# Row-tiled attention scores: two steps of 576 columns with an ordering fence, in place of three steps

## The chip, the core and the metric

One Trainium2 chip (trn2), one core. The metric is the device time of one execution in microseconds. The program runs on a single core, where most executions of one kernel agree within 0.3%, and the granted TensorE clock was 1.00 in the profiles before.

The profile's names: PE is the matrix engine and PEld its weight loads, ACT is ScalarE, DVE is VectorE, POOL is GpSimd, and a q behind a name (ACTq) means that engine's sequencer. `L279` is line 279 of the kernel at hand.

## The reference, cut to what matters

```python
k_p = k.reshape(B, H, 72, 8, 64).mean(axis=3)          # B=8, H=8, 576 tokens pooled to 72 keys
v_p = v.reshape(B, H, 72, 8, 64).mean(axis=3)
scores = q @ k_p.transpose(0, 1, 3, 2) / 8             # 576 x 72 per head
attn = softmax(scores)                                 # exp, then divided by the sum
x = attn @ v_p                                         # -> (B, 576, 512)
h = relu(x.T @ w_tok1) @ w_tok2 ; u = x + h.T          # mixing over tokens
out = u + relu(u @ w_ch1) @ w_ch2                      # mixing over channels, most of the work
```

## The kernel before

The PE runs `unit n`: the channel mixing of batch n in 48 steps, of two matmuls of 512 columns each (24 of `w_ch1`, 24 of `w_ch2`). Steps of the next batches are slipped in behind them by hand-written tables, such as `22: ">s0"`: behind step 22 of unit n, the score step s0 of batch n+2. `av`, `at`, `u`, `t` or `T` are the value, token-mixing and transposing steps that follow.

A score step multiplies four heads at once. The 64 numbers of a head are two halves (`db`) of 32, so each of the four row tiles (strips of 32 rows of the array, each with weights of its own) works on one head (`l`), in two rounds that accumulate:

```python
def score4(gs, n0, n):                       # before: s0, s1: one group of 4 heads, tokens 0 to 511
    pss = [ps_two.tile([P, 2, 512], FP32, name="p2") for _ in range(2)]        # s2: both groups, the last 64
    for i, g in enumerate(gs):
        for db in range(2):
            for l in range(4):
                quad = slice(l * 32, (l + 1) * 32)
                nc.tensor.matmul(out=pss[l // 2][0:SP, l % 2, i * n:(i + 1) * n], lhsT=st["kD"][quad, g, db, :],
                                 rhs=st["qD"][quad, g, db, n0:n0 + n],
                                 start=(db == 0), stop=(db == 1), tile_position=(l * 32, 0))
    ...
    for a in range(2):
        nc.scalar.activation(out=exv[...], in_=pss[a][...], func=AF.Exp, scale=scale)
```

PSUM is the memory that matmuls write. The kernel uses eight banks of it: two double ones (`p2`), three rotating single ones (`p1`, also for all large matmul groups) and one for transposes (`pt`). An eviction is an ACT instruction that reads a finished group of `w_ch1` out of its bank into the tile `GT`.

The softmax here doesn't subtract the row's maximum and nothing guards it: scores larger than these inputs give would overflow.

Of the kernel before, what the change touches and what calls it, by code (L numbers as in the profile page):

```python
# [8 lines left out]
FP32 = mybir.dt.float32  # L9
BF16 = mybir.dt.bfloat16  # L10
AF = mybir.ActivationFunctionType
# [3 lines left out]
DVE = mybir.EngineType.DVE  # L15
ACT = mybir.EngineType.Activation
SYNC = mybir.EngineType.SP


@with_exitstack  # L20
def kernel(
# [14 lines left out]
    nc = tc.nc  # L36
    B, H, S, D = q.shape
    P = 128
    POOL = 8
    SP = S // POOL  # L40
    BP, BR = 64, S // 64
# [8 lines left out]
    scale = 1.0 / (D ** 0.5) / POOL  # L50
# [9 lines left out]
    ps_one = ctx.enter_context(tc.tile_pool(name="ps_one", bufs=3, space=bass.MemoryType.PSUM))  # L60
    ps_two = ctx.enter_context(tc.tile_pool(name="ps_two", bufs=2, space=bass.MemoryType.PSUM))
    ps_tr = ctx.enter_context(tc.tile_pool(name="ps_tr", bufs=1, space=bass.MemoryType.PSUM))
# [93 lines left out]
    def batch_steps(b):  # L156

        par, first = b % 2, b == 0
        st = {}
# [85 lines left out]
        def qD(g, db):  # L245
            def go():
                st["qraw"] = quarters(loaded[b, "q"])
                nc.vector.transpose(  # L248
                    out=late("qD")[:, g, db].rearrange("m (r j u) -> m u r j", u=2, r=BR),
                    in_=st["qraw"][:, g].rearrange("m (u r d) -> m u r d", u=2, d=D)[:, :, :, db * 32:(db + 1) * 32])  # L250
            return go

        def score4(gs, n0, n):
            def go():
                pss = [ps_two.tile([P, 2, 512], FP32, name="p2") for _ in range(2)]
# [7 lines that stand above are left out]
                exv = st["ex"][:, 0:H * S].rearrange("j (g a l n) -> j a l g n", g=2, a=2, l=2)  # L263
                for a in range(2):
                    nc.scalar.activation(  # L265
                        out=exv[:, a, :, gs.start:gs.stop, n0:n0 + n],
                        in_=pss[a][0:SP, :, 0:len(gs) * n].rearrange("j l (g n) -> j l g n", n=n), func=AF.Exp, scale=scale)
            return go

        def score(hp, odd):  # L270
            n = OD if odd else EV

            def go():
                ps = ps_two.tile([P, 2, 512], FP32, name="p2")
                exv = st["ex"][:, 0:H * S].rearrange("j (h n) -> j h n", h=H)[:, 2 * hp:2 * hp + 2]
                for hl in range(2):
                    h = 2 * hp + hl
                    keys = slice(h * SP, (h + 1) * SP)
                    nc.tensor.matmul(out=ps[0:SP, hl, 0:n], lhsT=kT[:, odd, keys], rhs=qT0[:, hp, hl, 0:n],  # L279
                                     start=True, stop=True)  # L280
                dst = exv.rearrange("j h (r p) -> j h r p", p=BP)[:, :, odd:BR:2, :]
                src = ps[0:SP, :, 0:n].rearrange("j h (r p) -> j h r p", p=BP)
                nc.scalar.activation(out=dst, in_=src, func=AF.Exp, scale=scale)
            return go
# [182 lines left out]
        name = {"kpT": kpT}  # L467
# [5 lines left out]
        for hp in range(HP):  # L473
            name[f"kp{hp}"], name[f"kt{hp}"] = kp2(hp), kt2(hp)
            name[f"q{hp}"], name[f"o{hp}"], name[f"e{hp}"] = qT(hp), score(hp, 1), score(hp, 0)
        for i in range(4):
            name[f"Q{i}"] = qD(i // 2, i % 2)
        name["s0"], name["s1"], name["s2"] = (score4(range(0, 1), 0, 8 * BP), score4(range(1, 2), 0, 8 * BP),
                                              score4(range(2), 8 * BP, BP))
        for c in range(5):  # L480
            name[f"av{c}"], name[f"u{c}"], name[f"t{c}"] = av(c), u(c), uT(c)
            name[f"T{c}"] = blocks(c)
# [22 lines left out]
    def unit_steps(n, st):  # L505
# [36 lines left out]
        for a in range(2):  # L542
# [7 lines left out]
            for half in range(2):  # L550
# [9 lines left out]
             11: "lv3", 12: "kpT", 14: "s0", 15: "v1", 19: "s1", 25: "s2", 26: "av0", 27: "av1", 29: "av2",  # L560
             30: ">K1 av4", 31: "av3", 33: "at1", 34: "at0", 35: ">K0", 36: ">V1 u0", 37: "u1", 39: "t0 >V0",
             40: "u2", 41: "t1 u4 u3", 42: "t2", 44: "t3", 46: "t4"}
    SECOND = {0: ">K1 Q0 lq3 kpT Q1 Q2", 1: "lv3", 3: "s0 lk3 >V0", 4: ">K0", 6: "Q3 >V1", 8: "s1", 13: "s2",
              16: "av1 av0", 19: "av2", 20: "av3", 22: "av4", 24: "at1 at0", 26: "u0", 28: ">Q0", 29: "u1", 30: "t0",
              31: "u2", 32: "t1", 33: "u3 t2", 35: "t3", 36: ">Q1", 37: ">kpT", 38: "lq4", 39: ">s0 >Q2",
              40: ">Q3 lv4", 44: ">s1", 45: "lk4"}
    THIRD = {0: ">V0 >K1", 1: "s2", 2: ">K0 >V1", 3: "av0 av1", 6: "av3", 7: "av2", 9: "av4", 10: "at0",
             12: "at1 >Q0", 15: "u0", 16: "u1", 17: "u2 t0", 18: "u4", 19: "t1", 21: "u3", 22: "t2", 24: ">Q1",
             25: "t3", 27: "lq4 >kpT", 28: "lv4", 29: "lk4 >Q3 >s0 >Q2", 32: "t4", 33: ">s1", 38: ">s2", 40: ">av0",
             41: ">av2", 43: ">av1", 45: ">av3", 47: ">av4"}  # L570
    FOURTH = {0: "M4 u4 >K1", 1: "at0 at1 >K0", 3: "u0 >V0", 5: "u1 M0", 6: ">V1", 7: "u2", 8: "u3 M2", 9: "M",
              15: ">kpT >Q1", 17: ">Q0", 22: "lq4", 25: ">Q2", 26: ">s0", 27: "T0", 28: ">Q3 lk4 lv4", 29: "T1",
              32: ">s1 T2", 34: "T3", 37: ">s2", 38: "T4", 39: ">av0", 41: ">av1", 42: ">av2", 45: ">av3", 46: ">av4"}
    LATER = {0: ">K1 at0", 1: "at1", 2: ">V1", 3: "u1 >V0", 5: "u0 u2 u4 >K0", 7: "M0 M4", 9: "u3", 10: "M2", 11: "M",
             14: ">Q0", 17: ">Q1", 20: ">kpT", 22: ">s0", 25: ">Q2", 26: ">Q3", 27: "T0 >s1", 28: "T3", 31: "T2 T1",
             35: ">s2", 37: ">av1 >av0", 38: "T4", 41: ">av2", 45: ">av3", 46: ">av4"}
    warm = singles.tile([P, 512], BF16)

    def head(s):
# [10 lines left out]
    def unit(n, at):  # L590
        if n + 2 < B:
            batches[n + 2][0]()
        for i, _ in enumerate(unit_steps(n, batches[n][2] if n < B else None)):
            for s in at.get(i, "").split():
                if s[0] == "l":
                    load(s[1], n + int(s[2]))
                    continue
                ahead = {"<": 0, ">": 2}.get(s[0], 1)
                s = s.lstrip("<>")
                if n + ahead < B and ((n + ahead) % 2 or s not in ("u4", "t4", "M4", "T4")):  # L600
                    batches[n + ahead][1][s]()

    with tc.manual_schedule(engines={PE, POOLE, DVE, ACT, SYNC}):
        batches = [batch_steps(b) for b in range(B)]
        nc.vector.memset(warm, 0.0)
        for a in range(2):
# [21 lines left out]
        unit(0, FIRST)  # L628
        unit(1, SECOND)
        unit(2, THIRD)  # L630
        unit(3, FOURTH)
        for n in range(4, B + 1):
            unit(n, LATER)

# [29 lines left out]
```

## Time and profile before

| | before |
|---|---|
| time, median of the first 3 runs | 275.23 us |
| profiled span | 273.7 us |
| PE busy | 97% |
| a late unit, s0 of batch 6 to s0 of batch 7 (161.40 to 189.14) | 27.74 us |
| three score steps of a batch, with the way in and out | 0.65 + 0.65 + 0.36 us |
| PE waits over 0.1 us after the first 30 us, outside the score steps | three places, 0.66 us in all |

The prediction below shows the lines and how they are read.

### The profile page before, as it was taken

Reading aid. Unit: us, or ns where it says so; the run is one execution under the profiler, and the core shown is the slowest. Engines: PE = TensorE matmul, PEld = TensorE weight load, DVE = VectorE, ACT = ScalarE, POOL = GpSimd, SP = SyncE. Lnnn points to the kernel's source line nnn. Section 1 sums busy time; section 2 is a strip of 40 time slices with the busy share of each in tenths; the row PEclk is TensorE's granted clock in tenths of the full one; section 3 lists DMA queues with packets and bytes.
Section 4 is the critical chain, followed back from the end, with each engine's and each line's share of the span. In section 5 each row is a group of like instructions: output and inputs, shape, how many; then the busy total and the mean of one; then the engine's idle time right before and its main releaser. Section 6 shows DMA issues by size and latency. Waiting matters only on the chain.

```text
span 273.7 us, 4544 instructions
## 1 busy us (share of the span) xinstructions
PE 266.1 (97%) x1832; PEld 130.4 (48%) x1832; DVE 141.9 (52%) x280; ACT 110.4 (40%) x182; POOL 131.1 (48%) x121
## 2 busy tenths in 40 slices
PE   7799999999999999999999999999999999999994
PEld 3774545544453544454445444544454444444443
DVE  5487677862584666467267627753674062022022
ACT  2443690058306534525641484147413603603600
POOL 8685223999997991899099999300000000000000
PEclk9999999999999999999999999999999999999999
DMA  7999999990976920894399362225223634024024
GB/s 149 195 203 206 205 205 203 227 197 7 175 123 120 220 37 0 140 228 127 77 159 220 94 133 65 61 69 117 52 66 96 125 61 104 0 53 103 2 47 106
DMA packets 36837, 32.68 MB, mean 119 GB/s; under 512 B 14288, under 2 KB 30288, under 8 KB 36816
## 3 DMA queue, kind: packets, MB, share of 16 engines
q0 software_dynamic: 18672, 17.64, 40.7%
q1 hardware_dynamic: 17984, 14.62, 21.1%
q8 instruction: 14, 0.23, 0.3%
q10 hardware_dynamic: 160, 0.13, 0.2%
q14 instruction: 7, 0.06, 0.1%
HBM read 38.21 MB, written 11.80 MB: 183 GB/s over the span
## 4 chain that ended last, share of the span: by engine, by line
PE 89%; DMA 3%; ACT 3%; DVE 2%; POOL 1%; issue 1%; POOLq 0%
PE p L534 33%; PE p L512 32%; PE p L410 6%; PE p L395 6%; PE p L344 3%; PE p L260 3%; DMA vr<-in_v_dram 3%; ACT ex L265 1%; PE pt L420 1%; ACT GT L516 1%; PE p L226 1%; PE p L546 1%; POOL kr L86 1%; PE pt L376 1%; PE p L461 0%
## 5 line engine op out<-in xcount | busy, mean ns | idle before, releaser
L534 PE MATMUL p<-w_ch,GT 128*128 128x512 bf16 x420 | 101.5, 379 | 0.0
L512 PE MATMUL p<-uT,w_ch 128*128 128x512 bf16 x384 | 92.8, 379 | 0.1
L516 ACT ACTIVATE GT<-p 128x512 bf16<-128x512 f32 x108 | 63.8, 598 | 70.4 <-PE p L512 70.0
L512 PEld LDWEIGHTS <-w_ch 128*128 128x128 bf16 x432 | 40.6, 98 | 47.3 <-issue 2.5
L534 PEld LDWEIGHTS <-GT 128*128 128x128 bf16 x420 | 38.0, 98 | 42.0 <-issue 3.3
L520 DVE TENSOR_TENSOR o<-p,u 128x512 f32<-128x512 f32 x32 | 21.9, 685 | 31.6 <-PE p L534 31.2
L265 ACT ACTIVATE ex<-p 72x1024 bf16<-72x1024 f32 (+1 forms) x42 | 31.7, 807 | 13.5 <-PE p L260 13.5
L147 POOL TENSOR_TENSOR t<-t 72x512 f32<-72x512 f32 x24 | 30.4, 1265 | 1.9
L411 DVE TENSOR_TENSOR u<-p,x 128x512 bf16<-128x512 f32 x32 | 21.7, 690 | 14.7 <-PE p L410 14.4
L146 POOL TENSOR_TENSOR t<-kr 72x1024 f32<-72x1024 bf16 x12 | 25.5, 2123 | 6.7 <-DMA kr<-in_k_dram 6.0
L146 POOL TENSOR_TENSOR t<-vr 72x1024 f32<-72x1024 bf16 x12 | 25.5, 2124 | 0.8
L442 DVE STREAM_TRANSPOSE uT<-v 128x512 bf16<-128x512 bf16 x16 | 10.4, 688 | 23.4 <-DMA v<-mem 23.4
L248 DVE STREAM_TRANSPOSE qD<-qb 128x576 bf16<-128x576 bf16 x28 | 20.5, 794 | 0.4 <-DMA qb<-in_q_dram 0.4
L362 DVE TENSOR_TENSOR x<-p,den 128x512 bf16<-128x512 f32 x28 | 19.4, 692 | 1.0
L410 PE MATMUL p<-AT,w_tok 128*128 128x512 bf16 x64 | 18.4, 379 | 0.2 <-ACT GT L516 0.2
L386 ACT ACTIVATE AT<-p 128x512 bf16<-128x512 f32 x7 | 4.2, 597 | 32.2 <-PE p L395 32.2
L344 PEld LDWEIGHTS <-ex 72*128 72x128 bf16 x280 | 13.0, 98 | 7.9 <-DVE x L362 0.7
L356 DVE RECIPROCAL den<-p 128x8 f32<-128x8 f32 (+1 forms) x35 | 7.1, 202 | 15.9 <-PE p L344 15.4
L395 PE MATMUL p<-x,w_tok 128*128 128x512 bf16 x56 | 14.5, 379 | 0.0
L344 PE MATMUL p<-vp,ex 72*128 72x65 bf16 x280 | 14.1, 193 | 0.2 <-ACT ex L265 0.2
L104 POOL DMA_DIRECT2D qb<-in_q_dram x7 | 5.2, 739 | 17.8 <-DVE qD L248 16.2
L260 PE MATMUL p<-qD,kD 32*72 32x512 bf16 (+1 forms) x224 | 11.4, 294 | 0.1
(105 smaller groups left out, 205.4 us busy)
## 6 DMA issues: line engine op xcount, KB each, us to landing
out_dram<-o SPq DMA_DIRECT2D x70, 128.0 KB, 2.4
kr<-in_k_dram POOLq DMA_DIRECT2D x7, 576.0 KB, 13.8
qb<-in_q_dram POOLq DMA_DIRECT2D x7, 576.0 KB, 6.2
vr<-in_v_dram POOLq DMA_DIRECT2D x7, 576.0 KB, 14.1
w_ch<-in_moe_w_ch_dram POOLq DMA_DIRECT2D x6, 512.0 KB, 13.1
mem<-u SPq DMA_DIRECT2D x8, 256.0 KB, 2.1
v<-mem SPq DMA_DIRECT2D x8, 160.0 KB, 3.6
v<-mem SPq DMA_DIRECT2D x8, 128.0 KB, 3.1
```

The source lines that it names most:

```text
L146: eng.tensor_tensor(out=t4[:, 0:n], in0=t[:, hs, 0:4], in1=t[:, hs, 4:8], op=ALU.add)
L147: eng.tensor_tensor(out=t4[:, 0:n, 0:2], in0=t4[:, 0:n, 0:2], in1=t4[:, 0:n, 2:4], op=ALU.add)
L248: nc.vector.transpose(out=late("qD")[:, g, db].rearrange("m (r j u) -> m u r j", u=2, r=BR), in_=st["qraw"][:, g].rearrange("m (u r d) -> ...
L265: nc.scalar.activation(out=exv[:, a, :, gs.start:gs.stop, n0:n0 + n], in_=pss[a][0:SP, :, 0:len(gs) * n].rearrange("j l (g n) -> j l g n", ...
L344: nc.tensor.matmul(out=halves[h // 4][:, (h % 4) * (D + 1):(h % 4 + 1) * (D + 1)], lhsT=st["ex"][:, h * S + n0:h * S + n0 + P], rhs=st["vp ...
L395: nc.tensor.matmul(out=ps, lhsT=w_tok1[:, c if c < 4 else 4 + par, m * P:(m + 1) * P], rhs=st["x"][:, c, :] if c < 4 else st["xt"], start= ...
L410: nc.tensor.matmul(out=ps, lhsT=w, rhs=a, start=(i == 0), stop=(i == len(mms) - 1))
L411: nc.vector.tensor_tensor(out=dst, in0=ps, in1=x, op=ALU.add)
L512: nc.tensor.matmul(out=ps, lhsT=w_ch1[:, kk, m * P:(m + 1) * P], rhs=uT[:, kk, :], start=(kk == 0), stop=(kk == 3))
L516: nc.scalar.activation(out=GT[:, m, :], in_=ps, func=AF.Relu)
L520: nc.vector.tensor_tensor(out=o_sb, in0=ps, in1=(u_tails if n == B else st["u"])[:, c, :], op=ALU.add)
L534: nc.tensor.matmul(out=pss[c], lhsT=GT[:, m, c * P:(c + 1) * P], rhs=w_ch2[:, m, :], start=(m == 0), stop=(m == NM - 1))
```

## The change

For batches 3 to 7, s0 and s1 take all 576 tokens of their four heads, and s2 goes. A row tile then writes 512 columns in its bank of `p2` and 64 more elsewhere. Four such ends have two banks (`pt` and one `p1`), so tiles 0 and 2 share one, and tiles 1 and 3 the other. The kernel keeps two row tiles from writing one bank at once (the prediction names the page that asks for it): the ends of tiles 0 and 1 are issued first, those of 2 and 3 last, and a fence stands between. It is an ACT nop, an instruction that only waits and signals: it waits for the early ones, and the late ones wait for it. The tables of units 1 to 7 are written anew. Cut to its core:

```diff
+def score9(g):
+    main = [ps_two.tile([P, 2, 512], FP32, name="p2") for _ in range(2)]
+    tail = [ps_tr.tile([P, 512], FP32, name="pt"), ps_one.tile([P, 512], FP32, name="p1")]
+    def mm(l, db, n0, n): ...        # 512 columns to main[l // 2][.., l % 2], 64 to tail[l % 2][.., l // 2]
+    full, rest = (0, 8 * BP), (8 * BP, BP)
+    for db in range(2):
+        for l in (0, 1):
+            done = mm(l, db, *rest)                      # early short pieces
+        if db == 0:
+            for l in (2, 3):
+                mm(l, 0, *full)                          # long pieces, issued between them
+    fence = nc.scalar.nop()
+    tc.add_manual_dep(fence.ins, done.ins.name, ORDERED, reason="two row tiles write one bank")
+    for l, db in ((0, 0), (1, 0), (2, 1), (3, 1), (0, 1), (1, 1)):
+        mm(l, db, *full)
+    for db in range(2):
+        for l in (2, 3):
+            again = mm(l, db, *rest)                     # late short pieces
+            if (l, db) == (2, 0):
+                tc.add_manual_dep(again.ins, fence.ins.name, ORDERED, reason="two row tiles write one bank")
+    ...                                                  # exp: 2 of 1024 columns, 2 of 128
-name["s0"], name["s1"], name["s2"] = ...
+if b < 3:
+    name["s0"], name["s1"], name["s2"] = ...             # as before
+else:
+    name["s0"], name["s1"] = score9(0), score9(1)
...
-    LATER = {0: ">K1 at0", ... 14: ">Q0", 17: ">Q1", 20: ">kpT", 22: ">s0", ... 27: "T0 >s1", ... 35: ">s2", ...}
+    LATER = {0: ">V0", ... 17: ">Q0", 18: ">Q1 >kpT", 21: ">s0", ... 28: ">s1", 29: "T0", ...}
```

## The prediction

> **What bounds the kernel now.** I read the page's busy shares first, then the waits of the PE, then the PE's timeline around the scores of one late batch. The first view says that one engine is nearly always at work:
>
> ```profile
> PE 266.1 (97%) x1832; PEld 130.4 (48%) x1832; DVE 141.9 (52%) x280; ACT 110.4 (40%) x182; POOL 131.1 (48%) x121
> ```
>
> A busy PE need not be a PE at its pace, since matmul records overlap, so the pace is checked in the timeline (start, length, engine, line, operation, count). This is batch 6's score stretch, PE alone:
>
> ```profile
> 160.44 1.03 PE L512 MATMUL p<-uT,w_ch 128*128 128x512 bf16 x4
> 161.40 0.63 PE L260 MATMUL p<-qD,kD 32*72 32x512 bf16 x8
> 161.96 0.60 PE L512 MATMUL p<-uT,w_ch 128*128 128x512 bf16 x2
> 162.40 1.89 PE L534 MATMUL p<-w_ch,GT 128*128 128x512 bf16 x8
> 164.22 0.63 PE L260 MATMUL p<-qD,kD 32*72 32x512 bf16 x8
> 164.78 3.63 PE L534 MATMUL p<-w_ch,GT 128*128 128x512 bf16 x16
> 168.34 0.33 PE L260 MATMUL p<-qD,kD 32*72 32x64 bf16 x16
> 168.60 1.04 PE L534 MATMUL p<-w_ch,GT 128*128 128x512 bf16 x4
> 169.47 0.68 PE L344 MATMUL p<-vp,ex 72*128 72x65 bf16 x16
> ```
>
> Starts are the clock here. Four matmuls of L534 run from 168.60 to the next start at 169.47: 0.216 us each, that is 512 columns at about 2.4 columns per ns. The granted clock is 1.00 in every stretch. The 48 steps of a late unit are two times 48 such matmuls, 10 of L395 and 8 of L410 (114 x 0.216 = 24.6 us), plus 5 x 0.26 for L344, 0.13 for L195 and the scores (1.67, below): 27.7 us, and units repeat every 27.7 us (L195 at 160.31, then at 188.05). **So the late units have no stall to remove.** After the first 30 us the PE's list of waits holds two entries of 0.2 us each, one on the GT evictions and one on the exponentials. Only removing PE time, or adding a wait, can move the end.
>
> The three L260 lines are what the change replaces. Cost of each, from where the matmuls before it should have ended (count x 0.216) to the next start: 162.40 + 8 x 0.216 = 164.13, next L534 at 164.78: 0.65 us. The first, 160.44 + 4 x 0.216 = 161.30 to 161.96: 0.66. The 64-column one, 164.78 + 16 x 0.216 = 168.24 to 168.60: 0.36. Together **1.67 us a batch**. Batch 7 has the same starts one unit later (189.14, 191.96, 196.08).
>
> Of that, pure streaming is little. Eight matmuls in four row tiles are two rounds of 512 columns, 0.43 us; sixteen of 64 columns are four rounds, 0.107 us. The rest is the way in and out: about 0.22 us for each of the big ones and 0.25 us for the small one. The weight loads show the same at every score step, an idle of 0.42 us that no engine's wait explains:
>
> ```profile
> 164.22 0.15 PEld L260 LDWEIGHTS <-kD 32*72 32x72 bf16 x8 [0.42 <-issue]
> 164.78 3.14 PEld L534 LDWEIGHTS <-GT 128*128 128x128 bf16 x16 [0.41 <-issue]
> 168.34 0.22 PEld L260 LDWEIGHTS <-kD 32*72 32x72 bf16 x16 [0.42 <-issue]
> ```
>
> **What the Trainium skill says.** "TensorEngine Tiling (Array Packing)", Key Properties: changing the tiling mode drains the engine. The trace agrees in kind: the two 0.42/0.41 us pauses of the weight loads and the 0.22 to 0.25 us of lost PE time stand at each entry and exit of L260 and nowhere between L512 and L534. "TensorE: Matmul & The Clock Gate", Measured speedup vs the span model: four row tiles of 512 columns measured 3.07 times faster. Here 8 x 0.216 = 1.73 us became 0.56 us from start to next start, 3.1 times. "TensorEngine Tiling", Gotcha 1: different row tiles cannot access one PSUM bank at once and software must see to it; that is what the fence is for, and the kernel before never tests it, having one bank per row tile. "PSUM — Partial Sum Buffer", Engine vs sequencer instructions: a nop belongs to the sequencer, which waits only for earlier instructions to be dispatched, not completed. No trace here has such a nop, and the second rival hangs on it.
>
> **The change part by part, for batches 3 to 7.**
>
> (a) Removed: the third score step. It costs 0.36 us a batch, of which 0.25 is the mode change.
>
> (b) Added: each of the two remaining steps takes its own 64 last columns. Per row tile that is 2 x (512 + 64) = 1152 columns instead of 1024, 0.053 us more a step. The order issued starts the short pieces of tiles 0 and 1 beside the long pieces of 2 and 3 and mirrors that at the end. Walking it in issue order, with a start no earlier than its row tile is free, I get the fourth pair of long ones starting at 0.27 us and the last short ones at 0.46, ending at 0.49 us against an ideal 0.48. The weights are loaded as often as before (32 a batch), and the old 16-piece step shows short pieces are issued fast enough: 16 loads in 0.22 us. So a step becomes 0.65 + 0.06 = 0.71 us, and a batch 1.42 in place of 1.67: **0.25 us less, 1.25 us over five batches.**
>
> (c) ACT. The exponentials per batch were four of 1024 and two of 256 columns. The pairs' records say what each adds to the queue:
>
> ```profile
> 164.88 1.93 ACT L265 ACTIVATE ex<-p 72x1024 bf16<-72x1024 f32 x2 [0.41 <-PE p L260]
> 168.70 0.65 ACT L265 ACTIVATE ex<-p 72x256 bf16<-72x256 f32 x2 [1.89 <-PE p L260]
> ```
>
> A single one lasts 1.02 or 0.38 us, so the second adds 0.91 or 0.27. The slope is 0.64 us per 768 columns, so a 128-column one adds about 0.17 us (an estimate from these rows). Now a step queues 2 x 0.91 + 2 x 0.17 + a tail of 0.1 = 2.3 us, a batch about 0.4 us more than before. ACT is busy 40% and this alone costs nothing.
>
> (d) Buffers. A step now also takes one of the three rotating single banks and the transpose bank, and holds both until its last two exponentials, some 3.0 us after it starts. In the late units the next user of the single bank comes after the rest of L512 and a whole column block of L534 (12 x 0.216 = 2.6 us), about 4 us later: free. In unit 1, where batch 3's second step stands two matmuls before the unit ends, the bank is wanted at 0.57 + 0.43 + 2 x 0.86 + 0.52 = 3.2 us: just free. There the output block before it must also be added by DVE (0.69 us) one bank sooner than before; I allow 0.1 to 0.2 us once.
>
> (e) The fence: after the early short pieces, ACT runs a nop, and the late short pieces wait for it. The early ones start by 0.03 us and a 64-column record lasts 0.20 us, so they end at 0.23; the nop sees that some 0.03 us later (exponentials start 0.03 us after L260's modelled end: 162.03, 162.06), and from an ACT end to a PE start is about 0.1 us (the 256-column exponential at 39.83 plus 0.38 ends at 40.21, the waiting L344 starts at 40.30). I estimate arrival at 0.40 us, wanted at 0.43. **No wait, if ACT's queue is empty.**
>
> (f) The rest is the order of steps in units 1 to 7. There is little to win: in unit 1 the first score step takes 59.54 - 58.71 = 0.83 us instead of 0.56, because its second matmul round waits for the DVE transposes of q, which the new order starts earlier. I credit 0.2 us.
>
> Sum: -1.25 - 0.2 + 0.15 (buffers) = -1.3 us. I then add 0.2 us for the next rivals.
>
> **Rivals.** First, **the schedule is hit**: the moved transposes, spills and exponentials make a PE wait on DVE, DMA or a bank. For it: DVE is blocked up to 7.9 us at a time by the spilled transposes' loads, and the PE has no slack. Against it: the late order keeps those behind the output adds. It would cost 0.3 to 1 us, once or in every unit. Second, **the fence is late**, because the nop stands behind ACT work. In units 4 and 5 the first score step follows directly on a GT eviction of 0.60 us, which starts some 0.1 us after the step's start. If the nop completes only after it, the fence comes at 0.8 us instead of 0.40, a stall of 0.4 us in two or three places of ten: +0.8 to 1.2 us, leaving about 275.0. If every fence were late by 0.2 us, +2 us: about 276. The skill's page speaks against the first form. Third, **packing is worse than walked** (tiles 0 and 1 need three weights within 0.06 us): at most 0.1 us a step, 1 us in all, so no gain.
>
> **Range and chances.** 275.23 - 1.1 = **274.1 us**, a gain of 0.4%. With no loss at all and 0.6 us from the order: 273.0. With the fence late in a few places: 275.6. So 273.0 to 275.6 should hold it 8 times in 10. Faster by over 2% (below 269.7 us) would need 5.5 us where all score steps of the five batches cost only 8.4, 4.8 of it streaming: 1%. Slower by over 2% (above 280.7) would need over 0.6 us of stall at each of ten steps: 2%. Within 2%: 97%.
>
> **What would show it.** In the changed kernel's timeline each score step of batches 3 to 7 should be one group of 16 matmuls lasting 0.70 to 0.73 us from where the matmul before it ends to the next start, and no L260-like group of 64-column pieces should stand alone. The unit period should be 27.5 us instead of 27.7. A list of PE waits with ACT named at the score line would show the second rival; a group split in two by a pause, the late pieces apart, would show the fence in place; a wait of L512 on an exponential or an output add would show the first rival. The prediction is wrong if the score group takes over 0.85 us, or if any unit from 1 to 5 is longer than before.

## The result, and the profile after

The changed kernel took 275.09 us (median of 6 runs) beside 275.40 for the kernel before: ratio 0.9984, 95% interval 0.997 to 0.9999. Two later sets of runs gave 0.9993 (0.9981 to 1.0005) and 0.9987 (0.9964 to 1.001). A ratio here is the mean time of one kernel's fast runs over that of the other's of the same rounds, so it is not quite the ratio of the medians. The gain is some 0.2 to 0.4 us where 1.1 was predicted: within the range, but a fifth to two fifths of the size, and two of the three intervals do not exclude that there is none.

The busy shares, from the page, have hardly moved. ACT has ten instructions more, the PE the same count:

```profile
PE 265.8 (97%) x1832; PEld 131.6 (48%) x1832; DVE 141.7 (52%) x280; ACT 110.7 (41%) x192; POOL 130.9 (48%) x121
```

The start of the output addition that ends unit 0, and of the one that ends unit 7, bracket everything that the change touches and leave out the kernel's head, whose transfers vary from run to run. From DVE's timeline, before and then after:

```profile
56.96 0.69 DVE L520 TENSOR_TENSOR o<-p,u 128x512 f32<-128x512 f32 x1
...
249.22 0.69 DVE L520 TENSOR_TENSOR o<-p,u 128x512 f32<-128x512 f32 x1 [1.90 <-PE p L534]
```

```profile
56.68 0.69 DVE L560 TENSOR_TENSOR o<-p,u 128x512 f32<-128x512 f32 x1
...
248.73 0.69 DVE L560 TENSOR_TENSOR o<-p,u 128x512 f32<-128x512 f32 x1 [1.90 <-PE p L574]
```

That is 192.26 us before and 192.05 after: **0.21 us gained between the marks**. Now the score step itself. PE's timeline around the first step of batch 6; L279 is the new step's matmul, `pt` and `p` the banks it writes. A group has the shape of its first member, so "x3" and "x7" contain long pieces:

```profile
159.16 1.46 PE L552 MATMUL p<-uT,w_ch 128*128 128x512 bf16 x6
160.55 0.21 PE L279 MATMUL pt<-qD,kD 32*72 32x64 bf16 x1
160.55 0.41 PE L279 MATMUL p<-qD,kD 32*72 32x64 bf16 x3
160.60 0.19 PE L279 MATMUL pt<-qD,kD 32*72 32x64 bf16 x1
160.61 0.63 PE L279 MATMUL p<-qD,kD 32*72 32x64 bf16 x7
161.08 0.21 PE L279 MATMUL pt<-qD,kD 32*72 32x64 bf16 x1
161.09 0.21 PE L279 MATMUL p<-qD,kD 32*72 32x64 bf16 x1
161.14 0.19 PE L279 MATMUL pt<-qD,kD 32*72 32x64 bf16 x1
161.14 0.19 PE L279 MATMUL p<-qD,kD 32*72 32x64 bf16 x1
161.27 1.04 PE L552 MATMUL p<-uT,w_ch 128*128 128x512 bf16 x4
```

The six matmuls before it end at 159.16 + 6 x 0.216 = 160.46, the next one starts at 161.27: **0.81 us**, where the prediction has 0.71. The last four rows are the late short pieces, and a pause stands ahead of them. The weight loads of the same step name it (ACTq is ACT's sequencer, L289 the nop):

```profile
160.54 0.21 PEld L279 LDWEIGHTS <-kD 32*72 32x72 bf16 x12 [0.42 <-ACT GT L556]
161.08 0.14 PEld L279 LDWEIGHTS <-kD 32*72 32x72 bf16 x4 [0.32 <-ACTq L289]
```

Twelve weight loads go out in a row. The last four wait 0.32 us for the nop. In the compiled program the fence's wait stands on the weight load of the first late piece, so the weights cannot be brought in ahead either:

```
L279 Ldweights kD [waits Activation_sequencer]
L279 Matmult pt<-qD,kD 72x64
```

The nop's own record, and who waited for it, from the view of its line:

```profile
L289 ACTq EVENT_SEMAPHORE  x10: 17/17/17, 83.1 to 192.6; - x10
...
  PEld L279: 3.2, 10
```

Times inside a step, here and below, are read from the trace in nanoseconds and counted from the start of the step's first matmul. All ten steps are alike to 0.003 us: nop at 0.468 us, late weights at 0.536, late pieces at 0.537, next matmul at 0.722, and 0.093 on the way in. Two steps cost 1.63 us, where three cost 1.66 (1.69 in batch 4, whose second step took 0.02 us longer). Over five batches that is 0.17 us, nearly all of the 0.21 between the marks.

### The profile page after: what moved, and what is told of

It reads as the page before. It is cut to its first block, busy times and chain, and to the rows that moved or that the text cites. A ratio compares the mean times of both kernels' runs of the same rounds, so it can differ in the third digit from the quotient of the medians.

```text
span 273.3 us, 4565 instructions
## 1 busy us (share of the span) xinstructions
PE 265.8 (97%) x1832; PEld 131.6 (48%) x1832; DVE 141.7 (52%) x280; ACT 110.7 (41%) x192; POOL 130.9 (48%) x121
## 4 chain that ended last, share of the span: by engine, by line
PE 90%; ACT 3%; DVE 3%; DMA 2%; issue 1%; POOL 0%; POOLq 0%
PE p L574 33%; PE p L552 32%; PE p L447 6%; PE p L432 6%; PE p L381 3%; DMA kr<-in_k_dram 2%; PE p L279 2%; ACT ex L266 1%; PE pt L457 1%; ACT GT L556 1%; PE p L227 1%; PE p L586 1%; PE pt L279 1%; PE p L261 1%; PE p L205 1%
## 5 line engine op out<-in xcount | busy, mean ns | idle before, releaser
L300 ACT ACTIVATE ex<-p 72x1024 bf16<-72x1024 f32 x20 | 19.3, 1014 | 9.9 <-PE p L279 9.9
L381 PE MATMUL p<-vp,ex 72*128 72x65 bf16 x280 | 14.7, 194 | 0.2 <-ACT ex L266 0.2
L432 PEld LDWEIGHTS <-w_tok 128*128 128x128 bf16 x70 | 6.9, 98 | 8.4 <-issue 0.3
L198 ACT COPY kD<-pt 128x288 bf16<-128x288 bf16 x7 | 2.8, 398 | 19.6 <-PE pt L196 19.6
```

Source lines behind the costliest of these rows:

```text
L381: nc.tensor.matmul(out=halves[h // 4][:, (h % 4) * (D + 1):(h % 4 + 1) * (D + 1)], lhsT=st["ex"][:, h * S + n0:h * S + n0 + P], rhs=st["vp ...
L432: nc.tensor.matmul(out=ps, lhsT=w_tok1[:, c if c < 4 else 4 + par, m * P:(m + 1) * P], rhs=st["x"][:, c, :] if c < 4 else st["xt"], start= ...
```

## The experiments

My theory after this result: the fence is what the sum lacks. It is late because the notice that the early short pieces are done comes in the order in which matmuls were issued, so it waits for the two long pieces issued between them. Rivals: the new order of steps gives back what the steps gain; the row tiles themselves pack worse than I walked; ACT's sequencer is slow; or a signal simply takes that long.

In the traces of the first eight experiments 31 matmul records of an execution are missing (1801 of 1832 are there). A step whose follower is missing looks 0.22 us longer; such steps are read without it.

### The new order with the old steps

```diff
-        if b < 3:
+        if b < 8:
-    THIRD = {0: ">V1", 1: ">K1", ... 36: ">s1", 40: ">av0", ...}
+    THIRD = {0: ">V1", 1: "s2 >K1", ... 36: ">s1", 39: ">s2", 40: ">av0", ...}
     # likewise ">s2" at 37 in FOURTH and 35 in LATER
```

> The new order of steps with the old three score steps (the third one put back just before the value steps). The record of the changed kernel shows 0.815 us for each new score step, so 1.63 us a batch against 1.66 before: the steps explain 0.17 us over five batches. Theory (the step is the mis-sized term, the order is worth the rest): faster than before by 0.1 to 0.4 us, ratio 0.9985 to 0.9997. Rival (the steps win their 1.25 us and the new order gives most of it back): slower than before by 0.5 us or more, ratio 1.002 to 1.004.

Measured: 277.34 us, ratio 1.0062 (1.0049 to 1.0075), as the rival had it in sign and more. But the trace puts it on a thing that I built in:

```profile
113.94 0.22 PE L261 MATMUL p<-qD,kD 32*72 32x64 bf16 x2
114.63 0.32 PE L261 MATMUL p<-qD,kD 32*72 32x64 bf16 x14 [0.47 <-ACT ex L266]
```

The old third step needs the double banks that the second step's exponentials still hold. I put it three slots behind the second, where the old order had five. Its later pieces start 0.69 us after its first; batch 3's third step shows the same. These two waits are 1.4 us of the 1.55 lost between the marks. In the units after, mark to mark from unit 2 to 5, it took 205.12 - 119.84 = 85.28 us, the kernel before 203.84 - 118.84 = 85.00: no gain from the order in these units. So the run says that the new order has no room for a third step; what the order alone is worth in the early units stays open.

### The new steps in the old order

```diff
-    (the new SECOND, THIRD, FOURTH, LATER)
+    (those of the kernel before, without the s2 of batches 3 to 7)
```

> The new score steps in the old order of steps, the old third step left out. Theory: each step takes 0.815 us here too, the whole is 0.1 to 0.3 us faster than before, ratio 0.999 to 1.000, unless the banks held longer make a matmul wait in the old order, which would show as a wait of L552 or L574 and up to 0.5 us more. Rival: 1 us or more faster, ratio 0.9965 or less.

Measured: 276.51 us, ratio 1.0048 (1.0029 to 1.0068): slower, so the expected gain missed and the added "unless" came true, larger than I had allowed. The steps themselves took 0.815 us where nothing else held them, as in the changed kernel. The loss is mostly one place, again a bank:

```profile
110.34 0.27 ACT L302 ACTIVATE ex<-pt 72x128 bf16<-72x128 f32 x1
110.50 0.28 ACT L302 ACTIVATE ex<-p 72x128 bf16<-72x128 f32 x1
110.66 0.38 PE L457 MATMUL pt<-ident,u_tails 128*128 128x128 bf16 x4 [0.69 <-ACT ex L302]
```

The transpose of unit 2's tails wants bank `pt`, which the score step three slots earlier handed to ACT until its last but one exponential: 0.69 us of idle PE in this view, and 0.85 by starts (the five matmuls from 108.73 should have ended at 109.81). That is most of the 1.02 us lost between the marks. The changed kernel's table puts these six slots apart, and the same transpose there follows its neighbours without a wait. This is the first rival of the prediction, and the new order is the answer to it. The two parts of the change are worth nothing apart, in these forms.

### Long pieces cut in two, short ones between the halves

```diff
-for db in range(2):
-    for l in (0, 1):
-        done = mm(l, db, *rest)
-    if db == 0:
-        for l in (2, 3):
-            mm(l, 0, *full)
+for l in (0, 1): mm(l, 0, *rest)
+for l in (2, 3): mm(l, 0, 0, 4 * BP)                # 256 columns
+for l in (0, 1): done = mm(l, 1, *rest)
+for l in (2, 3): mm(l, 0, 4 * BP, 4 * BP)           # start=False for this half
```

> The first long pieces of row tiles 2 and 3 are cut into two of 256 columns, and the early short pieces are issued between the halves. Theory (a matmul's completion is told in issue order, so the fence waits for the two long pieces issued ahead of the short ones): the nop runs at about 0.36 us after the start of the step instead of 0.47, the late pieces start when their row tile is free, at 0.48 to 0.50 instead of 0.54, the step falls from 0.72 to 0.67 to 0.70 us from first start to next start, and the total by 0.2 to 0.5 us against the changed kernel. Rival (the semaphore path takes a fixed 0.41 us from the short piece): nop at 0.47, late pieces at 0.54, no gain, or a loss by the two added matmuls.

Measured: 274.52 us, ratio 0.9957 (0.9944 to 0.997), beside 0.9993 for the changed kernel in the same set: 0.9 us less by the medians and between the marks (191.18), 1.0 by the ratios. What changed is how much long work is issued ahead of the last early short piece; two matmuls were even added. The wait ahead of the late weights shrank from 0.32 to 0.17 us:

```profile
160.97 0.26 PEld L279 LDWEIGHTS <-kD 32*72 32x72 bf16 x14 [0.42 <-ACT GT L558]
161.41 0.15 PEld L279 LDWEIGHTS <-kD 32*72 32x72 bf16 x4 [0.17 <-ACTq L291]
161.60 0.55 PEld L554 LDWEIGHTS <-w_ch 128*128 128x128 bf16 x4
```

The nop ran at 0.362 us instead of 0.468. The 0.106 us between them are the 256 columns by which the pieces issued ahead became shorter (256 at 2.4 columns per ns is 0.107). The late pieces started at 0.469 and the step took 0.627 us, more than hoped for. A fixed signal time is ruled out.

The changed kernel ran again beside it:

> The changed kernel as it is, once more on the same chip, as the yardstick for the other three: ratio 0.997 to 0.9995 against before, score steps 0.72 us from first start to next start, all ten alike.

Measured: 275.40 us, ratio 0.9993 (0.9981 to 1.0005), steps as before, and 192.06 us between the marks.

### Four banks for the ends, no fence

```diff
-tail = [pt, p1]            # two tiles a bank
+tail = [pt, p1, p1, p1]    # one tile a bank; the fence and both its dependencies go, four exps of 64 columns
```

> Each row tile's last 64 columns get a bank of their own (all eight banks are then in use at a step), so no fence is needed and there is none. The whole will be slower, as the matmul groups before and after wait for banks; only the inside of the score steps counts. Theory (the fence costs the part of the step between 0.48 and 0.54 us): the weights of the late pieces are loaded without a pause, the late pieces start at 0.47 to 0.49 us, first start to next start is 0.66 to 0.68 us where nothing waits. Rival (the row tiles' own order and weights set the step): late pieces still at 0.53 us or later and 0.72 us.

Measured: 306.79 us in one look (state unknown, clock 0.972), as the matmul groups have no bank left. Inside the step it tells what was asked. Batch 6's first:

```profile
179.94 0.36 PEld L279 LDWEIGHTS <-kD 32*72 32x72 bf16 x14 [0.42 <-ACT GT L551]
179.94 0.21 PE L279 MATMUL pt<-qD,kD 32*72 32x64 bf16 x1
```

Fourteen weight loads go out with no pause, and the first late piece, the only one that no bank keeps waiting, starts at 0.466 us in all the steps (two at 0.465). So packing gives 0.466, the fence 0.537. The step's whole length cannot be read here, as the other late pieces wait for banks; that half of the expectation is not tested.

### All short early pieces first

```diff
 for db in range(2):
     for l in (0, 1):
         done = mm(l, db, *rest)
-    if db == 0:
-        for l in (2, 3):
-            mm(l, 0, *full)
+for l in (2, 3):
+    mm(l, 0, *full)
```

> All four early short pieces are issued ahead of the first long ones. Theory (completion told in issue order): the nop runs at 0.25 to 0.32 us after the start instead of 0.47 and the fence is no longer waited for; but the long pieces of row tiles 2 and 3 start 0.056 us later, so the step stays at 0.70 to 0.74 us. Rival (fixed 0.41 us from the last short piece): nop at 0.45 us or later.

Measured: 275.83 us in one look, after a head of 58.3 us to the first mark (56.6 to 57.6 elsewhere); between the marks 191.23. The nop ran at 0.293, as expected. The step did not stay at 0.72 but fell to 0.631: my walk had the long pieces of tiles 2 and 3 start 0.056 us later, behind the second short pair, and they did not. Timed, with the changed kernel beside it on one chip:

> The kernel of the untimed look, now timed. Its ten steps took 0.63 us instead of 0.72 from first start to next start, so 10 x 0.09 = 0.9 us less than the changed kernel is expected if a step's time comes out one to one: ratio to before 0.995 to 0.9975, and the changed kernel beside it 0.998 to 1.000. Rival (the saved time is waited for elsewhere): no difference between the two, both at 0.998 to 1.000.

> The changed kernel on the same chip, as the yardstick: ratio to before 0.998 to 1.0005.

Measured: 274.47 us, ratio 0.9955 (0.9931 to 0.9979), and 275.28 us, 0.9987 (0.9964 to 1.001) for the changed kernel. The marks agree: 57.17 to 248.39, 191.22 us, 0.83 less than the changed kernel and 1.04 less than the kernel before. The same step, PE and then weight loads:

```profile
160.57 0.21 PE L279 MATMUL pt<-qD,kD 32*72 32x64 bf16 x1
160.57 0.41 PE L279 MATMUL p<-qD,kD 32*72 32x64 bf16 x3
160.63 0.19 PE L279 MATMUL pt<-qD,kD 32*72 32x64 bf16 x1
160.63 0.63 PE L279 MATMUL p<-qD,kD 32*72 32x64 bf16 x7
161.04 0.19 PE L279 MATMUL pt<-qD,kD 32*72 32x64 bf16 x1
...
161.20 1.04 PE L551 MATMUL p<-uT,w_ch 128*128 128x512 bf16 x4
```

```profile
160.57 0.59 PEld L279 LDWEIGHTS <-kD 32*72 32x72 bf16 x16 [0.42 <-ACT GT L555]
```

All sixteen weight loads now stand in one group, with no pause put down to the nop, and the view of the nop's line lists nobody who waited for it. In the trace the late weights still follow it, at 0.359 us, but that is 0.11 us before their pieces start at 0.473, so the fence costs nothing. And the order of starts is worth a look. Issued are `pt`, `p`, `pt`, `p` (short), then two long `p`. Started are `pt` and three `p` (one of 0.41 us from first start to last end, so long ones among them), and only then the second `pt`. In the trace the long ones start at 0.014, the short ones issued ahead of them at 0.056 and 0.059. Those short ones start at 0.056 and 0.059 in the changed kernel too, with the long ones at 0.007 and 0.010. **Up to the last long pieces the array does the same work at the same times in both, to 0.007 us; only the order of issue differs, and the nop comes at 0.468 or at 0.293.**

The trace also holds the moment at which the semaphore that the nop waits for is raised. In the compiled programs it is raised by the last early short piece itself, and this piece starts at 0.058 to 0.060 us in all three kernels. The semaphore is raised at 0.447 us in the changed kernel, where two pieces of 512 columns are issued ahead of it, at 0.341 with two of 256 columns ahead, and at 0.273 with none, to 0.001 us in all ten steps. So the delay lies between the matmul and its semaphore, before any other engine has a part in it. That is the mechanism: completion is told in order of issue.

### The nop on another engine, and work in place of the nop

```diff
-fence = nc.scalar.nop()
+fence = nc.gpsimd.nop()
```

> The nop runs on GpSimd instead of ACT. Theory (the fence is late because of the completion of the matmuls, not because of ACT): in batch 7, where GpSimd has nothing to do, the nop runs at 0.45 to 0.50 us as before and the step takes 0.71 to 0.74 us; in earlier batches it may be later, behind GpSimd's own work. Rival (ACT's sequencer delays it): nop below 0.40 us in batch 7 and a step under 0.69 us.

Measured: 276.00 us in one look; late pieces at 0.540 us in nine steps and 0.553 in one, steps of 0.726 (0.739). ACT is not what makes the fence late. The early batches, where GpSimd has work of its own, were no later, which I had thought possible.

```diff
-fence = nc.scalar.nop()
+fence = nc.scalar.copy(out=mark[:, 1:2], in_=mark[:, 0:1])      # one column
```

> The fence is a real one-column ACT copy instead of the nop, so it stands in the engine's own order behind any GT eviction. Theory (the nop passes work in flight): in batches 6 and 7 the first step, which follows on a GT eviction that ends 0.70 us after its start, now releases the late pieces at 0.9 to 1.0 us, a step of 1.05 to 1.2 us; in the other eight, where ACT is idle or done by then, the copy adds some 0.2 us, a step of about 0.9 us. Total 2 to 3 us slower than the changed kernel, which also tells whether PE time added in a step comes out one to one. Rival (the nop already waits for work in flight, or PE time there is hidden): all ten steps alike, or the total unchanged.

Measured: 277.64 us, ratio 1.0095 (1.007 to 1.012). Steps took 0.955 us in seven places, 0.899 in one, and 1.022 in the two that follow on a GT eviction, where the copy stands behind it:

```profile
161.94 0.60 ACT L556 ACTIVATE GT<-p 128x512 bf16<-128x512 f32 x1 [0.27 <-PE p L552]
162.43 0.18 ACT L289 COPY mark<-mark 128x1 f32<-128x1 f32 x1
```

In the changed kernel the same eviction runs from 0.107 to 0.704 us of the step, and the nop at 0.468 in the midst of it: a nop passes work in flight, a copy does not. This agrees with the Trainium skill, "PSUM — Partial Sum Buffer", Engine vs sequencer instructions: a nop is the sequencer's, which waits only until the instructions before it are dispatched. The ten steps are 7 x 0.233 + 0.177 + 2 x 0.300 = 2.41 us longer than the changed kernel's, and between the marks (56.71 to 251.08) the run took 194.37 us, 2.32 more. **A step's time comes out nearly one to one.** My lengths were a little off, above the measured 1.02 for the two and below 0.955 for most of the others.

| kernel | nop or copy done, us from the step's start | late weights | late pieces start | step, first start to next matmul | between the marks |
|---|---|---|---|---|---|
| changed | 0.485 | 0.536 | 0.537 | 0.722 | 192.05 |
| long pieces cut | 0.379 | 0.429 | 0.469 | 0.627 | 191.18 |
| short first | 0.310 | 0.359 | 0.473 | 0.631 | 191.22 |
| four banks, no fence | none | 0.252 | 0.466 | not to be read | - |
| copy as fence (most steps) | 0.717 | 0.767 | 0.769 | 0.955 | 194.37 |

In every kernel with a fence the late weights come 0.05 us after it is done. Where that is at 0.36 or 0.43 us, the row tiles are the limit (0.47), so a still earlier fence should bring nothing.

## Why the prediction was right or wrong

**What bounds the kernel** was right: the PE, at pace, so that 2.4 us added in steps came out as 2.3, and 0.9 us removed as 0.83. One reading on the way was loose: of the two waits that it lists after the first 30 us, the one on a GT eviction ends at 25.91 us, and two pauses that show by starts alone (0.15 us at 45.50, 0.19 at 80.47) are not in it.

**(a), the third step removed**, was right: 0.36 us a batch, with no step of short pieces left alone.

**(b), the packing**, was right too, though the changed kernel could not show it. I had 0.71 us for a step. Without a fence in the way it is 0.631 + 0.093 = 0.72, and the unit period is 188.09 - 160.57 = 27.52 us, the 27.5 that I named (27.70 in the changed kernel, 27.74 before). That is in the short-first order of issue. In the order that I walked, the run without a fence shows only the first late piece, at 0.466. The starts of the walk were 0.04 us early (fourth long pair at 0.313 for 0.27, last short ones at 0.50 for 0.46), which did not enter the sum, as 0.71 is the old step's 0.65 plus 0.06. One reason in it was wrong without consequence: long pieces of tiles 2 and 3 do not wait for short ones of tiles 0 and 1 that were issued earlier.

**(e), the fence, is the step that failed**: "I estimate arrival at 0.40 us, wanted at 0.43. **No wait, if ACT's queue is empty.**" The late weights came at 0.536, wanted for a start at 0.47. The sum's term for the fence was nought and measured 0.722 - 0.631 = 0.091 us a step, 0.9 us in ten, against a predicted gain of 1.1. Two things were missing in the estimate. The short pieces' end was taken from their own record (0.23 us), as if nothing issued ahead of them mattered; it moves the nop from 0.293 to 0.468, and the first late piece from 0.473 to 0.537, which is 0.064 of the 0.091. And the wait stands on a weight load, so the late weights are not ready beforehand. The other 0.027 is that the late pieces then start in pairs 0.055 us apart, against 0.028 in the short-first kernel; that the weight load is the reason is argued, as no run puts the wait elsewhere. The passage quoted first in the list at the end has matmuls end in order of issue; the prediction cites that page and did not use it.

**(f), 0.2 us from the order**, was not there in the place named: batch 2's first step still takes 59.26 - 58.43 = 0.83 us. Another wait is gone instead, the transpose that started 0.19 us late at 80.47 in the kernel before, and three small ones came (0.08 and twice 0.06 us). **(d), the buffers**, allowed 0.15 and measured 0.08 us at the turn of unit 1, in the way foreseen: the matmul at 88.18 waits for the output addition that ends at 88.12. It is one of the three just named. **(c), ACT**, has a batch about 0.4 us longer (4.6 with two tails after, 4.2 without any before); busy time rose from 110.4 to 110.7 us, 0.06 a batch. It cost nothing, as said.

**The rivals.** The second, a late fence, is what happened, but in a third form: not behind ACT work in a few places (0.4 us each), which the copy shows that a nop avoids, but by some 0.07 us in all ten. I had priced 0.2 in all ten at 2 us and given it too little weight. The first, a hit on the schedule, did not happen in the changed kernel; the old order shows that it would have (0.85 us by starts). The third, packing, fell. The mark that I set for being wrong, a group over 0.85 us, was too lax: 0.81 sufficed to lose most of the gain. The other mark, a unit longer than before, was too strict: by the start of its first `w_ch1` matmul, unit 1 went from 30.57 to 30.75 us, as the work of batch 3's third step moved into it from unit 2 (31.42 to 31.14). The ends of the range do not follow from the sums either: "no loss at all and 0.6 us from the order" gives 275.23 - 1.25 - 0.6 = 273.4 and not 273.0, and a fence late in a few places "about 275.0" in one paragraph and 275.6 in another.

## What to carry to other kernels

Put the signal's producer ahead of long work in issue order. In these runs a matmul's completion is told in order of issue, so here the semaphore of a short piece was as late as the long pieces issued before it, though the array ran them side by side. Here a few lines swapped made the fence free and turned a gain of 0.1 to 0.2% into 0.45%. And estimate a fence as notice of the last piece issued ahead, plus the hop to the other engine and back (here 0.447 us to 0.536), plus a weight load if it holds one back, not from the short piece's own record.

## What the Trainium skill lacked or had wrong

- "TensorE: Matmul & The Clock Gate", The mechanism, has matmuls "pc-monotone in start AND end". For the end the runs agree: the nop comes at 0.468, 0.362 and 0.293 us as the pieces issued ahead of the short ones have 512, 256 and no columns. For the start they do not: in the short-first kernel long pieces of other row tiles start at 0.014 us, short ones issued before them at 0.056.
- "TensorEngine Tiling (Array Packing)", Gotcha 1, says that software must keep two row tiles off one bank, and has no cost for it: 0.09 us a step in the changed kernel, none to be seen where the signal was issued early.
- No page says that a wait on a matmul may stand on its weight load, so that it also stops the load from running ahead: late weights at 0.536 us, their pieces at 0.537 us.
